# Padding tile rows and ring buffers by 32 and 64 bytes, and moving one small buffer into a ring

## The chip, the cores and the metric

The kernel runs on one core of a Trainium2 chip. The metric is the device time of one execution in microseconds (us), as the median of the runs. The engines are TensorE (PE, with its weight loads as PEld), VectorE (DVE), ScalarE (ACT), GpSimd (POOL) and SyncE (SP), which issues the DMAs.

## The reference, cut to what matters

```python
batch, n_heads, seq, head_dim = (8, 8, 576, 64); n_features = 128      # attention
n_tokens, d_model, d_ff = (4608, 512, 2048)                           # two dense layers, float32 in, float64 weights

def phi(x):                                    # x is q or k, scaled
    h = einsum('bhsd,md->bhsm', x, omega) - sum(x * x, -1) / 2
    return exp(h - max(h, -1)) / sqrt(m)
q_p, k_p = phi(q_s), phi(k_s)
kv = einsum('bhsm,bhsd->bhmd', k_p, v)
z = sum(k_p, axis=2)
attn = einsum('bhsm,bhmd->bhsd', q_p, kv) / (einsum('bhsm,bhm->bhs', q_p, z)[..., None] + 1e-06)

x = attn.transpose(0, 2, 1, 3).reshape(4608, 512)
h = x @ w_in                                   # 512 -> 2048
g = where(h > 0, h, exp(minimum(h, 0)) - 1)
out = g @ w_out                                # 2048 -> 512
```

## The kernel before

The work is recorded as tasks with a cost and a due time. A planner in `Plan.order` simulates the engines, takes on each engine the ready task with the earliest due time, and so writes one fixed order for every engine; the pools' rings (how many buffers a tag has) are part of what it simulates.

All large products use float32 in a form that TensorE takes in one pass and that keeps fewer bits, so each operand is kept as a head (the rounded value) and a tail (what is left). A product is three matmuls: head with head, head with tail, tail with head. In the table below, the moving operand of a matmul is the one that streams through the array, one column after the other, and the other, 128x128, is loaded before as weights; each matmul has its own weight load, which runs beside the matmul before it.

There are three kinds of long streams.

- **Layer 1** (`layer1`, L969 to L971): the weights are blocks of `w1c`, a ring of 3 buffers with 1024 floats each for heads and for tails; the moving operand is 384 columns of `xh` (heads of x) or `xl` (tails). Twelve matmuls make one 128x384 block of h.
- **Layer 2** (`layer2`, L1003 to L1005): the weights are 128x128 pieces of `g`, a ring of 6 buffers; the moving operand is a row `w2h[:, f]` or `w2l[:, f]` of 512 columns.
- **The last form** (`wide1` and `wide2`, L1354, L1324 and L1512): the last 1536 tokens are computed with seven products in place of eight (combined quarter matrices), all with 256 moving columns. Weights are `wp` (in the ring `w1c`), `wq` (in the ring `u`) and `gq` (in the ring `g`; the first product's g has the one buffer `gx` to itself). Moving operands are units kept in `xh` and `xl`, quarters of `w2h` and `w2l`, and combined quarters that `rooms` puts into buffers of other tags (`ld`, `t`, `v`, `qh`, `raw`, `zs`) which the attention no longer needs.

Beside these, the attention projects q and k (`project`, L541): the moving operand is `om`, 256 columns, the weights are blocks of `tk` or `tq`, which lie in the ring `t`.

Three pools share SBUF. Tiles of `const` (`w2h`, `w2l`, `xh`, `xl` among them) come one after the other, then the rings of `sb` in the order in which their tags are first used. So the size of one tile moves every later tile.

Of the kernel before, what the change touches and what calls it, by code (L numbers as in the profile page):

```python
# [9 lines left out]
F32 = mybir.dt.float32  # L10
# [8 lines left out]
P = 128  # L19
# [9 lines left out]
NTT = TB // P  # L29
NBLK = 8  # L30
TOK0 = NBLK * TB
# [36 lines left out]
LAG = 3.4  # L68

# [35 lines left out]
class Buf:  # L105
# [213 lines left out]
def performer_elu_kernel(  # L319
# [41 lines left out]
    w2h = const.tile([P, NF, DM], F32R, name="w2h")  # L361
# [6 lines left out]
    xh = const.tile([P, NC, RING], F32R, name="xh")  # L368
# [587 lines left out]
    def layer1(F, due):  # L956
# [4 lines left out]
        e = Buf(sb, [P, TB], F32, "e", f"e_{F}", 2)  # L961
        g = gt[F] = [Buf(sb, [P, 512], F32R, "g", f"g_{F}_{z}", 6) for z in range(2)]

        def ph():
            return p()[:, 0:TB]

        def mms(c):
            wh, wl = w()[:, 0, c * P:(c + 1) * P], w()[:, 1, c * P:(c + 1) * P]
            nc.tensor.matmul(ph(), wh, xh[:, c, o:o + TB], start=(c == 0), stop=False)  # L969
            nc.tensor.matmul(ph(), wh, xl[:, c, o:o + TB], start=False, stop=False)  # L970
            nc.tensor.matmul(ph(), wl, xh[:, c, o:o + TB], start=False, stop=(c == NC - 1))  # L971

        for c in range(NC):
            reads = [("x3h", SLOT[blk], c), ("x3l", SLOT[blk], c)] if blk > 2 else [(z, k) for k in ring(blk) if k[1] == c for z in ("xh", "xl")]
            op("PE", mm(TB, 3), due + 0.5 * c, lambda c=c: mms(c), [*reads, (w, "h"), (w, "l")], (p, ("f", blk, f)) if c == 0 else (p, ("fl", blk, f)) if c == 3 else (p,))
        due += 2

        op("ACT", act(TB, True), due, lambda: nc.scalar.activation(e(), ph(), AF.Relu, scale=-1.0), (p,), (e,))  # L978
        op("ACT", act(TB), due + 0.2, lambda: nc.scalar.activation(e(), e(), AF.Exp, scale=-1.0), (e,), (e,))  # L979
        op(  # L980
            "DVE", dve(TB), due + 0.8,
            lambda: nc.vector.scalar_tensor_tensor(ph(), e(), -1.0, ph(), ALU.add, ALU.max), (p, e), (p,),  # L982
        )
        first, second = ("ACT", act(TB, True)), ("DVE", dve(TB))
        if blk:
            first, second = second, first
        op(*first, due + 1.2, lambda x: copy(x, g[0]()[:, 0:TB], ph()), (p,), (g[0],), alt=other("g_hi", *second))
        op(
            "DVE", dve(TB), due + 1.5,
            lambda: nc.vector.tensor_tensor(g[1]()[:, 0:TB], ph(), g[0]()[:, 0:TB].bitcast(F32), ALU.subtract),  # L990
# [3 lines left out]
    def layer2(F, due):  # L994
        blk, f, f0, f1 = STEPS[F]
        g = gt.pop(F)
        for tt in range(NTT):
# [14 lines left out]
            r = blk * TB + tt * P  # L1012
# [174 lines left out]
    def std_x(blk, due):  # L1187

        X = [Buf(sb, [P, NJ, M], F32, "h", f"xs_{blk}_{k}", 4) for k in range(2)]

        def x(k):
            return X[k]().rearrange("p j x -> p (j x)")[:, 0:2 * TB].rearrange("p (c x) -> p c x", c=2)

        t0, o = blk * TB, SLOT[blk] * TB
        for k in range(2):
            op(
                "SP", 500, due + 0.1 * k,
                lambda k=k: nc.sync.dma_start(x(k), xd[2 * k:2 * k + 2, :, t0:t0 + TB].rearrange("c p x -> p c x")),
                [("xd", b * NHP + hp) for b in range(B) if b * S < t0 + TB and t0 < b * S + S for hp in (2 * k, 2 * k + 1)]
                + [("f", blk - 1, 11)], (X[k],), P * TB * 8,  # L1200
# [3 lines left out]
            xk = [z[:, 2 * k:2 * k + 2, o:o + TB] for z in (xh, xl)]  # L1204
            heads, tails = ([(nm, SLOT[blk], c) for c in (2 * k, 2 * k + 1)] for nm in ("x3h", "x3l"))
            op(
                "ACT", act(2 * TB), due + UNIT0 + 0.5 * k, lambda e, k=k, xk=xk: copy(e, xk[0], x(k)), (X[k],),
                [*(("xh", z) for z in keys), *heads], alt=other("unit_hi", "DVE", dve(2 * TB, True)), port=True,
            )
            op(  # L1210
                "POOL", pool(2 * TB), due + UNIT0 + 0.4 + 0.5 * k,
# [490 lines left out]
```

## Time and profile before

| | |
|---|---|
| median of 2 runs | 1010.52 us (1010.38 to 1010.66) |
| span of the profiled execution, first to last instruction | 1006.4 us |
| own time of the profiled execution | not listed apart from the two runs; the span is 4.1 us under their median |
| instructions in the span | 24315 |
| PE, PEld busy | 981.2 us (97%), 883.9 us (88%) |
| DVE, ACT, POOL busy | 842.0, 765.8, 557.6 us |
| granted clock of TensorE | full speed (2.4 GHz) in all 40 slices of the page |

The span is what the trace shows; the 4.1 us around it are start and end of the execution. A matmul's duration in the trace holds its way through the array as well as its columns, and matmuls overlap. So what a matmul costs in a stream is the distance from its start to the next start, and the durations tell how two groups of the same shape differ.

### The profile page before, as it was taken

Reading aid. Unit: us, or ns where it says so; the run is one execution under the profiler, and the core shown is the slowest. Engines: PE = TensorE matmul, PEld = TensorE weight load, DVE = VectorE, ACT = ScalarE, POOL = GpSimd, SP = SyncE. Lnnn points to the kernel's source line nnn. Section 1 sums busy time; section 2 is a strip of 40 time slices with the busy share of each in tenths; the row PEclk is TensorE's granted clock in tenths of the full one; section 3 lists DMA queues with packets and bytes.
Section 4 is the critical chain, followed back from the end, with each engine's and each line's share of the span. In section 5 each row is a group of like instructions: output and inputs, shape, how many; then the busy total and the mean of one; then the engine's idle time right before and its main releaser. Section 6 shows DMA issues by size and latency. Waiting matters only on the chain.

```text
span 1006.4 us, 24315 instructions
## 1 busy us (share of the span) xinstructions
PE 981.2 (97%) x7806; PEld 883.9 (88%) x7806; DVE 842.0 (84%) x3077; ACT 765.8 (76%) x2064; POOL 557.6 (55%) x745
## 2 busy tenths in 40 slices
PE   7999999999999999999999999999999999999997
PEld 7788788878888888888888888888789999999997
DVE  7999977887778788878888888889999889779766
ACT  7989777777668888888787778776546788777774
POOL 2667666685547767677577766684442232223221
PEclk9999999999999999999999999999999999999999
DMA  7656787757776776676666766767878876766752
GB/s 230 174 191 198 232 276 262 249 185 236 232 246 202 236 229 204 210 240 207 223 211 220 237 196 211 231 218 236 295 272 309 294 264 205 233 219 193 220 200 66
DMA packets 93264, 226.27 MB, mean 225 GB/s; under 512 B 23056, under 2 KB 35024, under 8 KB 93136
## 3 DMA queue, kind: packets, MB, share of 16 engines
q1 hardware_dynamic: 93136, 224.70, 68.8%
q8 instruction: 63, 1.03, 0.4%
q14 instruction: 65, 0.53, 0.2%
HBM read 187.43 MB, written 37.22 MB: 223 GB/s over the span
## 4 chain that ended last, share of the span: by engine, by line
PE 68%; DVE 15%; DMA 6%; ACT 5%; issue 3%; POOL 3%; SPq 1%; DVEq 0%; POOLq 0%; ACTq 0%
PE acs L1512 9%; PE ph L969 6%; PE ph L971 6%; PE acc L1003 6%; PE ph L970 6%; PE A L1354 6%; PE acc L1005 6%; PE acc L1004 6%; PE B L1354 4%; PE pkv L609 2%; PE pn L829 2%; PE ppq L541 2%; PE ppk L541 2%; DVE junk L727 1%; DVE u_w L914 1%
## 5 line engine op out<-in xcount | busy, mean ns | idle before, releaser
L969 PE MATMUL ph<-xh,w1c 128*128 128x384 f32 x512 | 176.9, 345 | 6.3 <-DVE g L990 4.4
L970 PE MATMUL ph<-xl,w1c 128*128 128x384 f32 x512 | 172.3, 336 | 1.0 <-DVE xl L794 1.0
L971 PE MATMUL ph<-xh,w1c 128*128 128x384 f32 x512 | 172.3, 336 | 0.0
L1003 PE MATMUL acc<-w2h,g 128*128 128x512 f32 x384 | 154.6, 402 | 0.1
L1005 PE MATMUL acc<-w2h,g 128*128 128x512 f32 x384 | 151.6, 395 | 0.0
L1004 PE MATMUL acc<-w2l,g 128*128 128x512 f32 x384 | 151.3, 394 | 0.0
L969 PEld LDWEIGHTS ph<-xh,w1c 128*128 128x128 f32 x512 | 96.2, 188 | 18.7 <-DVE g L990 8.5
L970 PEld LDWEIGHTS ph<-xl,w1c 128*128 128x128 f32 x512 | 96.3, 188 | 3.8 <-DVE xl L794 1.4
L978 ACT ACTIVATE e<-ph 128x384 f32<-128x384 f32 x128 | 62.5, 488 | 47.5 <-PE ph L971 47.0
L381 POOL TENSOR_TENSOR hq<-hq,den 128x512 f32<-128x512 f32 (+1 forms) x96 | 80.9, 852 | 28.7 <-DVE den L736 23.2
L971 PEld LDWEIGHTS ph<-xh,w1c 128*128 128x128 f32 x512 | 96.2, 188 | 0.0
L982 DVE SCALAR_TENSOR_TENSOR ph<-e,ph 128x384 f32<-128x384 f32 x128 | 71.3, 557 | 27.4 <-ACT e L979 26.1
L381 POOL TENSOR_TENSOR gq<-yh,gq 128x256 fp32r<-128x256 f32 x49 | 42.8, 873 | 87.0 <-ACT gq L376 76.8
L1005 PEld LDWEIGHTS acc<-w2h,g 128*128 128x128 f32 x384 | 72.0, 188 | 17.1
L1003 PEld LDWEIGHTS acc<-w2h,g 128*128 128x128 f32 x384 | 72.1, 188 | 16.2 <-issue 6.3
L727 DVE CUSTOM_DVE_ANT_0 junk<-hq,pz 128x128 f32<-128x128 f32 (+1 forms) x320 | 74.6, 279 | 12.7 <-PE pz L705 10.6
L381 POOL TENSOR_TENSOR tk<-xk,tk 64x576 fp32r<-64x576 f32 x45 | 64.1, 1424 | 32.2 <-ACT tk L376 14.9
L461 ACT ACTIVATE hk<-hk,nbk 128x128 f32<-128x128 f32 x216 | 68.4, 391 | 15.7 <-POOL nbk L567 15.3
L1004 PEld LDWEIGHTS acc<-w2l,g 128*128 128x128 f32 x384 | 72.2, 188 | 8.7
L461 ACT ACTIVATE hq<-hq,nbq 128x128 f32<-128x128 f32 x216 | 68.4, 391 | 13.5 <-POOL nbq L567 13.0
L381 POOL TENSOR_TENSOR tq<-xq,tq 64x576 fp32r<-64x576 f32 x46 | 65.9, 1432 | 21.4 <-ACT tq L376 11.1
L990 DVE TENSOR_TENSOR g<-ph,g 128x384 fp32r<-128x384 f32 x128 | 70.6, 551 | 5.7 <-PE pn L829 1.8
(222 smaller groups left out, 2816.9 us busy)
## 6 DMA issues: line engine op xcount, KB each, us to landing
w1c<-w1s SPq DMA_DIRECT2D x112, 512.0 KB, 4.4
wp<-w1t SPq DMA_DIRECT2D x48, 512.0 KB, 3.7
raw_w<-in_w_dram SPq DMA_DIRECT2D x32, 512.0 KB, 4.3
xk<-in_kx_dram SPq DMA_DIRECT2D x24, 576.0 KB, 4.6
xq<-in_qx_dram SPq DMA_DIRECT2D x24, 576.0 KB, 4.6
wp<-w1s SPq DMA_DIRECT2D x24, 512.0 KB, 4.2
v<-in_v_dram SPq DMA_DIRECT2D x32, 325.0 KB, 3.2
w1s<-w1c SPq DMA_DIRECT2D x16, 512.0 KB, 3.9
```

The source lines that it names most:

```text
L381: (nc.vector if e == "DVE" else nc.gpsimd).tensor_tensor(*args)
L461: nc.scalar.activation(h()[:, j, :], src(j), AF.Exp, bias=nb()[:, j:j + 1], scale=-1.0)
L727: nc.vector.tensor_tensor_reduce(out=junk()[r], in0=h()[r, j, :], in1=pz()[r, a * P:(a + 1) * P], scale=1.0, scalar=EPS, op0=ALU.mult, op1 ...
L969: nc.tensor.matmul(ph(), wh, xh[:, c, o:o + TB], start=(c == 0), stop=False)
L970: nc.tensor.matmul(ph(), wh, xl[:, c, o:o + TB], start=False, stop=False)
L971: nc.tensor.matmul(ph(), wl, xh[:, c, o:o + TB], start=False, stop=(c == NC - 1))
L982: lambda: nc.vector.scalar_tensor_tensor(ph(), e(), -1.0, ph(), ALU.add, ALU.max), (p, e), (p,),
L1003: nc.tensor.matmul(a(), g[0]()[:, ts], w2h[:, f], start=(f == f0), stop=False)
L1004: nc.tensor.matmul(a(), g[0]()[:, ts], w2l[:, f], start=False, stop=False)
L1005: nc.tensor.matmul(a(), g[1]()[:, ts], w2h[:, f], start=False, stop=(f == f1 - 1))
L1354: nc.tensor.matmul(o, at(a, i), u[b][:, i], start=(start and fresh_bank and i == 0 and n == 0), stop=(i == 1 and n == 2), skip_group_check ...
L1512: nc.tensor.matmul(bank()[:, z * TH:(z + 1) * TH], g()[:, a * TH + z * P:a * TH + z * P + P], w(b), start=(j == 0 and z == 0 and m == 0), ...
```

## The change

Rows of `w2h` get 8 floats more (32 bytes), of which no one reads the last 8; the same for rows of `xh`. A tile of 64 bytes, `gap`, that no one uses stands between `w2h` and `w2l`. Buffers of the tags `w1c` and `g` get 16 floats more (64 bytes). In the last form the g of the first product takes a buffer of the ring `g`, whose 6 buffers so serve seven g's a step in place of six, and the tag `gx` is gone. The rest of the diff writes the block size as a list in place of one number; all blocks stay 384 tokens.

```diff
+PAD = dict(w1c=16, g=16)
+ROW = 8
...
         if self.tile is None:
             pool, shape, dtype, name = self.args
-            self.tile = pool.tile(shape, dtype, tag=self.key, bufs=self.n, name=name)
+            pad = PAD.get(self.key, 0)
+            if pad:
+                size = 1
+                for n in shape[1:]:
+                    size *= n
+                t = pool.tile([shape[0], size + pad], dtype, tag=self.key, bufs=self.n, name=name)[:, 0:size]
+                self.tile = t if len(shape) == 2 else t.rearrange("p (a x) -> p a x", a=shape[1])
+            else:
+                self.tile = pool.tile(shape, dtype, tag=self.key, bufs=self.n, name=name)
...
-    w2h = const.tile([P, NF, DM], F32R, name="w2h")
+    w2h = const.tile([P, NF, DM + ROW], F32R, name="w2h")[:, :, 0:DM]
+    const.tile([P, 2 * ROW], F32, name="gap")
     w2l = const.tile([P, NF, DM], F32R, name="w2l")
...
-    xh = const.tile([P, NC, RING], F32R, name="xh")
+    xh = const.tile([P, NC, RING + ROW], F32R, name="xh")[:, :, 0:RING]
     xl = const.tile([P, NC, RING], F32R, name="xl")
...
-            tag, n = ("gx", 1) if p == 1 else ("g", 6)
+            tag, n = ("g", 6)
```

The built programs place the tiles at these bytes of a partition. Offsets inside a tile that a matmul starts at are multiples of 256 bytes, but for the rows of the padded tiles, so the start modulo 256 is what the change moves.

| tile | role in a matmul | start before | modulo 256 | start after | modulo 256 |
|---|---|---|---|---|---|
| `om` | moving, projection | 17024 | 128 | 17024 | 128 |
| `w2h` | moving | 19584, rows of 2048 | 128 | 19584, rows of 2080 | 128, 160, 192, 224, 0, 32, 64, 96 in turn |
| `w2l` | moving | 52352 | 128 | 52928 | 192 |
| `xh` | moving | 85120, rows of 4608 | 128 | 85696, rows of 4640 | 192, 224, 0, 32 |
| `xl` | moving | 103552 | 128 | 104256 | 64 |
| `ld` | moving, last form | 123008 | 128 | 123712 | 64 |
| `t` | weights, projection; moving, last form | 132224 | 128 | 132928 | 64 |
| `qh`, `raw` | moving, last form | 146688, 156928 | 0 | 147392, 157632 | 192 |
| `u` (`wq`) | weights | 188800 | 128 | 189504 | 64 |
| `w1c` (`wp`) | weights | 195136, 4096 apart | 64 | 195840, 4160 apart | 0, 64, 128 |
| `g` (`gq`) | weights | 210624, 2048 apart | 192 | 211520, 2112 apart | 64, 128, 192, 0, 64, 128 |
| `gx` | weights | 227264 | 192 | gone | |

Up to the start of the last form every engine has the same instructions in the same order. From there the planner's order differs, since the ring `g` now holds one g more. The first place is on PE, at the head of the last form; `acs` are the banks of the second layer's products, and the number triples are step, product and the buffer's running number. Before:

```order
L1354 MATMUL B<-xh,wp_1_0_11541 128x256 x6
L1512 MATMUL acs_11654<-w2h,gq_0_1_11616 128x256
L1512 MATMUL acs_11654<-w2l,gq_0_1_11616 128x256
L1512 MATMUL acs_11654<-w2h,gq_0_1_11616 128x256 x2
L1512 MATMUL acs_11654<-w2l,gq_0_1_11616 128x256
L1512 MATMUL acs_11654<-w2h,gq_0_1_11616 128x256
L1354 MATMUL A<-xl,wp_1_1_11568 128x256 x6
L1324 MATMUL A<-w2h,gq_0_2_11630 128x256
L1324 MATMUL A<-w2l,gq_0_2_11630 128x256
L1324 MATMUL A<-w2h,gq_0_2_11630 128x256
L1354 MATMUL B<-xl,wp_1_1_11568 128x256 x6
```

The same place on PE after:

```order
L1369 MATMUL B<-xh,wp_1_0_11542 128x256 x6
L1369 MATMUL A<-xl,wp_1_1_11569 128x256 x6
L1339 MATMUL A<-w2h,gq_0_2_11628 128x256
L1339 MATMUL A<-w2l,gq_0_2_11628 128x256
L1339 MATMUL A<-w2h,gq_0_2_11628 128x256
L1527 MATMUL acs_11672<-w2h,gq_0_1_11631 128x256
L1527 MATMUL acs_11672<-w2l,gq_0_1_11631 128x256
L1527 MATMUL acs_11672<-w2h,gq_0_1_11631 128x256 x2
L1527 MATMUL acs_11672<-w2l,gq_0_1_11631 128x256
L1527 MATMUL acs_11672<-w2h,gq_0_1_11631 128x256
L1369 MATMUL B<-xl,wp_1_1_11569 128x256 x6
```

The first product's second-layer matmuls (`gq_0_1`) stand nine matmuls later, behind one product of the next step and half of the second product's.

The second place is on ACT at the same time, where the heads of the g's are written. Before:

```order
L1402 ACTIVATE yh<-c_0_0_11562 128x256
L376 CAST gq_0_1_11616<-yh 128x256
L1407 ACTIVATE yh<-yh 128x256
L376 COPY o_0_0_11625<-acc_0_0_10738 128x512
L376 CAST gq_0_2_11630<-y_0_10_11588 128x256
L1402 ACTIVATE y_0_01_11636<-c_0_0_11534 128x256
```

And after:

```order
L1417 ACTIVATE yh<-c_0_0_11563 128x256
L389 COPY o_0_0_11617<-acc_0_0_10739 128x512
L1422 ACTIVATE yh<-yh 128x256
L389 CAST gq_0_2_11628<-y_0_10_11589 128x256
L389 CAST gq_0_1_11631<-yh 128x256
L1417 ACTIVATE y_0_01_11638<-c_0_0_11535 128x256
```

The first product's g (`gq_0_1`) is written three instructions later, behind the second product's, since it now waits its turn in the ring.

## Rows read from the trace of the kernel before

**Rows 1.** The page, engines: busy us (share of the span) xinstructions.

```profile
PE 981.2 (97%) x7806; PEld 883.9 (88%) x7806; DVE 842.0 (84%) x3077; ACT 765.8 (76%) x2064; POOL 557.6 (55%) x745
```

**Rows 2.** Stretches: us, busy (x) by engine, PEclk, DMA share, GB/s.

```profile
300.00:500.00 200.00, 199.25 (x1756) 175.16 (x1756) 164.21 (x793) 167.22 (x471) 141.37 (x216) 1.00 0.70 220
...
790.00:860.00 70.00, 69.68 (x605) 69.39 (x604) 61.04 (x155) 56.20 (x158) 21.34 (x26) 1.00 0.75 246
```

**Rows 3.** PE's waits, 0 to 790 us: total us, times, longest.

```profile
PE ph L969 <- DVE g L990: 4.4, 8, 1.5
```

**Rows 4.** PE's waits, 790 us to the end, all of them.

```profile
PE A L1354 <- DMA wp<-w1t: 1.2, 1, 1.2
PE acs L1512 <- DVE gq L381: 0.3, 1, 0.3
```

**Rows 5.** By source line: count, duration ns min/median/max, first and last start us.

```profile
L970 PE MATMUL ph<-xl,w1c x512: 332/336/445, 59.0 to 756.3; 128*128 128x384 f32 x171
...
L971 PE MATMUL ph<-xh,w1c x512: 331/336/340, 59.2 to 756.4; 128*128 128x384 f32 x171
...
L1004 PE MATMUL acc<-w2l,g x384: 388/394/398, 72.2 to 769.5; 128*128 128x512 f32 x192
...
L1005 PE MATMUL acc<-w2h,g x384: 388/394/400, 72.4 to 769.7; 128*128 128x512 f32 x192
```

**Rows 6.** Timeline of PE at 698 us: start us, us, instruction.

```profile
698.38 0.39 PE L1004 MATMUL acc<-w2l,g 128*128 128x512 f32 x1
698.62 0.39 PE L1005 MATMUL acc<-w2h,g 128*128 128x512 f32 x1
698.84 0.40 PE L1003 MATMUL acc<-w2h,g 128*128 128x512 f32 x1
...
699.54 0.34 PE L969 MATMUL ph<-xh,w1c 128*128 128x384 f32 x1
...
700.06 0.33 PE L969 MATMUL ph<-xh,w1c 128*128 128x384 f32 x1
...
703.70 0.39 PE L1003 MATMUL acc<-w2h,g 128*128 128x512 f32 x1
```

**Rows 7.** By source line, matmuls of 256 columns, columns as in rows 5.

```profile
L541 PE MATMUL ppk<-om,tk x216: 274/281/359, 109.8 to 670.3; 128*128 128x256 f32 x108
...
L1354 PE MATMUL A<-xh,wp x240: 276/276/357, 758.0 to 986.3; 128*128 128x256 f32 x120
...
L1354 PE MATMUL A<-xl,wq x96: 278/283/384, 764.3 to 991.1; 128*128 128x256 f32 x96
...
L1512 PE MATMUL acs<-w_raw,gq x108: 276/279/384, 834.2 to 1000.1; 128*128 128x256 f32 x108
L1512 PE MATMUL acs<-w_qh,gq x90: 279/279/281, 803.4 to 980.1; 128*128 128x256 f32 x90
...
L1512 PE MATMUL acs<-w_t,gq x72: 276/276/281, 784.5 to 960.5; 128*128 128x256 f32 x72
```

**Rows 8.** Timeline of PE at 926 us, columns as in rows 6.

```profile
926.61 0.87 PE L1512 MATMUL acs<-w_raw,gq 128*128 128x256 f32 x6
927.32 0.87 PE L1354 MATMUL B<-xl,wp 128*128 128x256 f32 x6
928.03 0.87 PE L1354 MATMUL A<-xh,wp 128*128 128x256 f32 x6
...
929.07 0.84 PE L1512 MATMUL acs<-w_ld,gq 128*128 128x256 f32 x6
929.75 0.28 PE L1512 MATMUL acs<-w2h,gq 128*128 128x256 f32 x1
```

**Rows 9.** Tile gq, 790 us to the end: durations; then idle before its instructions.

```profile
L376 ACT CAST gq<-yh x83: 389/407/412, 790.5 to 996.9; 128x256 fp32r<-128x256 f32 x83
...
L381 POOL TENSOR_TENSOR gq<-yh,gq x45: 723/747/1355, 789.5 to 992.6; 128x256 fp32r<-128x256 f32 x45
...
  PE acs L1512: 1.9, 6
```

More of the change, by code (lines that the diff above doesn't have):

```diff
@@ L28 @@
 TB = 384
-NTT = TB // P
-NBLK = 8
-TOK0 = NBLK * TB
+BLOCKS = [TB] * 8
+NBLK = len(BLOCKS)
+START = [sum(BLOCKS[:n]) for n in range(NBLK + 1)]
+TOK0 = START[-1]
 SB = 512
@@ L976, in layer1 @@
         due += 2
-        op("ACT", act(TB, True), due, lambda: nc.scalar.activation(e(), ph(), AF.Relu, scale=-1.0), (p,), (e,))
-        op("ACT", act(TB), due + 0.2, lambda: nc.scalar.activation(e(), e(), AF.Exp, scale=-1.0), (e,), (e,))
-        op(
-            "DVE", dve(TB), due + 0.8,
-            lambda: nc.vector.scalar_tensor_tensor(ph(), e(), -1.0, ph(), ALU.add, ALU.max), (p, e), (p,),
+        op("ACT", act(n, True), due, lambda: nc.scalar.activation(e()[:, 0:n], ph(), AF.Relu, scale=-1.0), (p,), (e,))
@@ L983, in layer1 @@
+        op("ACT", act(n), due + 0.2, lambda: nc.scalar.activation(e()[:, 0:n], e()[:, 0:n], AF.Exp, scale=-1.0), (e,), (e,))
+        op(
+            "DVE", dve(n), due + 0.8,
+            lambda: nc.vector.scalar_tensor_tensor(ph(), e()[:, 0:n], -1.0, ph(), ALU.add, ALU.max), (p, e), (p,),
         )
-        first, second = ("ACT", act(TB, True)), ("DVE", dve(TB))
+        first, second = ("ACT", act(n, True)), ("DVE", dve(n))
         if blk:
             first, second = second, first
-        op(*first, due + 1.2, lambda x: copy(x, g[0]()[:, 0:TB], ph()), (p,), (g[0],), alt=other("g_hi", *second))
+        op(*first, due + 1.2, lambda x: copy(x, g[0]()[:, 0:n], ph()), (p,), (g[0],), alt=other("g_hi", *second))
@@ L996, in layer2 @@
         g = gt.pop(F)
-        for tt in range(NTT):
+        for tt in range(BLOCKS[blk] // P):
             if f == f0:
@@ L1203, in std_x @@
             keys = [z for z in ring(SLOT[blk]) if z[1] in (2 * k, 2 * k + 1)] if first else []
-            xk = [z[:, 2 * k:2 * k + 2, o:o + TB] for z in (xh, xl)]
+            xk = [z[:, 2 * k:2 * k + 2, o:o + n] for z in (xh, xl)]
             heads, tails = ([(nm, SLOT[blk], c) for c in (2 * k, 2 * k + 1)] for nm in ("x3h", "x3l"))
             op(
-                "ACT", act(2 * TB), due + UNIT0 + 0.5 * k, lambda e, k=k, xk=xk: copy(e, xk[0], x(k)), (X[k],),
-                [*(("xh", z) for z in keys), *heads], alt=other("unit_hi", "DVE", dve(2 * TB, True)), port=True,
+                "ACT", act(2 * n), due + UNIT0 + 0.5 * k, lambda e, k=k, xk=xk: copy(e, xk[0], x(k)), (X[k],),
+                [*(("xh", z) for z in keys), *heads], alt=other("unit_hi", "DVE", dve(2 * n, True)), port=True,
             )
             op(
-                "POOL", pool(2 * TB), due + UNIT0 + 0.4 + 0.5 * k,
+                "POOL", pool(2 * n), due + UNIT0 + 0.4 + 0.5 * k,
                 lambda e, k=k, xk=xk: tt(e, xk[1], x(k), xk[0].bitcast(F32), ALU.subtract), (X[k], *heads),
-                [*(("xl", z) for z in keys), *tails], alt=other("unit", "DVE", dve(2 * TB)), port=True,
+                [*(("xl", z) for z in keys), *tails], alt=other("unit", "DVE", dve(2 * n)), port=True,
             )
```

28 lines of the change are left out of this document (15 added, 13 removed).

## The prediction, before the changed kernel ran

> **What bounds the kernel now.** I read the page's engine line first. PE is busy 97% of the span, DVE 84%, and nothing else comes near [rows 1]. Then the stretches: from 300 to 500 us PE is busy 199.25 of 200 us, and in the last form 69.68 of 70, at full clock in both [rows 2]. Then PE's waits, for whether that busy time is broken up: ahead of 790 us the largest is 4.4 us in 8 pieces, and in the last form there are 1.5 us in all [rows 3, 4]. So matmuls set the time, and a change that leaves their number alone can act only through how far apart their starts lie, or by making waits.
>
> So the next view is the timeline, for the distance of starts. In a row of 21 matmuls of 384 columns it is 3.64 us / 21 = 173.3 ns, and for 512 columns 0.70 us / 3 = 233.3 ns [rows 6]. At 2.4 GHz, one column a cycle, 384 and 512 columns take 160.0 and 213.3 ns. So 13.3 and 20.0 ns of each matmul are neither columns nor waits. The same for 256 columns: six matmuls from `w_ld` take 0.68 us, 113.3 ns each, six from `w_raw` 0.71 us, 118.3 ns [rows 8]; the columns alone take 106.7 ns.
>
> These extra ns depend on which tiles are read. Same shape, same line, only other buffers: the median is 276 ns with `w_t` or with `xh` and `wp`, 279 with `w_raw` and `w_qh`, 283 with `xl` and `wq`, 281 with `om` and `tk` [rows 7]. Beside the table of start bytes that reads: moving at 128 and weights at 64 or 192 (modulo 256) give 276; moving at 0 gives 279; both at 128 give 281 to 283. It also has a memory: six matmuls of `xl` and `wp` right behind `w_raw` keep 118 ns (0.71 us for six), and after `w_ld` the distance is 113 again [rows 8]. Almost all of layer 1 and 2 has moving 128 with weights 64 or 192, so for the long streams the trace of before shows one placing alone.
>
> **The change part by part.** The padded floats are read by no one, the number of instructions is the same, and no transfer gets longer. What remains is four terms.
>
> *Projection (L541).* 432 matmuls read `om` at 128 and weights at 128, median 281. Their weights move to 64, a pair that shows 276 elsewhere [rows 7]: 432 x -5 ns = -2.2 us, of which I count -2, since PE is busy 199.25 of 200 us there [rows 2].
>
> *The last form.* There are 1008 + 864 + 144 = 2016 matmuls of 256 columns here. From the operands of the two programs I count those whose moving start and whose next weights are equal modulo 256: 156 before, 444 after. At 7 ns each (283 against 276, rows 7) the 288 more cost +2.0 us. Another 198 leave the place 0 (279 to at best 276): -0.6. In 407 the moving start becomes an odd multiple of 32, for which no row has a price: 0 in the middle, and 7 ns either way would be 2.8 us. Sum +1.
>
> *The long streams.* 1536 matmuls of 384 columns and 1152 of 512. All of them get other starts, and no row has a price. The bounds: below, all of the extra goes, 1536 x 13.3 + 1152 x 20.0 = 20.4 + 23.0 = -43 us; above, each takes the 7 ns that a coinciding pair costs at 256 columns: 2688 x 7 = +19 us. Inside that, the nearest rows are these streams' own fastest: minimum 331 against median 336, and 388 against 394 [rows 5]. These are met at the start of a stream (0.22 us from 698.62 to 698.84 at 512 columns, then 233 in the settled run, rows 6), that is, where the start offset has just changed or the stream has just begun. Now heads and tails start at different offsets and the rows of heads differ among themselves by 32 bytes, so a stream is in that state more often. If all reached the minimum it were 1536 x 5 + 1152 x 6 = 14.6 us; I take half, -7. That is a choice between bounds and no measurement.
>
> *The ring and the order.* In the last form seven g's a step share 6 buffers. What could be late is a g's head on ACT and its tail on POOL, 407 and 747 ns [rows 9], behind the release of a buffer. Instructions that write or read a g waited 1.9 us in all for PE's second-layer matmuls, 6 times in the whole stage [rows 9], PE waited 0.3 us for a g [rows 4], and the new order puts the first product's matmuls nine matmuls later, which gives that g more time. Queued behind such a wait on ACT are the next heads and the copies out of the banks, for which PE waits. I put it at 0; the cover is that PE has other products to run meanwhile, and without it the price is in the fourth case below. SP's weight loads change places by one or two in the queue only.
>
> Sum: -2 + 1 - 7 + 0 = -8 us. The profiled span is 1006.4 us, and the median 4.1 us above it; nothing in the change touches start or end, so 998.4 + 4.1 = 1002.5 us.
>
> **The rivals.** *Nothing moves.* The extra ns of the long streams may belong to their length: 6.7, 13.3 and 20.0 ns at 256, 384 and 512 columns grow by the same 6.7 ns for each 128 columns, as a cost tied to columns would. Then only the first two terms are left, which is 1009.5; I give 1007 to 1014. For it speaks that straight line, against it that at 256 columns placing does count (276 against 283, rows 7). The Trainium skill would have it so too: SBUF — State Buffer, section "SBUF: two separate sides", says that on the engine side only the port shared by VectorE and GpSimd causes contention and that PE waits for no one. By that page padding is worth nothing at all and the time is 1010.5; rows 7 disagree with it by 7 ns a matmul, for 256 columns.
>
> *The extra goes.* If what costs is two streams that meet in one place, and rows 32 bytes apart keep them from meeting, most of the 43 us can go; at 0.7 of it, -30 us, the time is 980. For it speaks that placing costs at all; against it that starts coincide more often after the change than before (444 against 156 in the last form). [...]
>
> *They meet more often* (slower). The same mechanism with the other sign, in layers 1 and 2: before, nearly all pairs there are in the best class that the trace shows. After, `xl` at 64 meets `w1c`'s second buffer at 64, `w2l` at 192 meets `g`'s third at 192, and a state lasts into matmuls behind it [rows 8]. If half of the 2688 take 7 ns more that is +9.4, with the last form's +1 and the projection's -2 some +9: 1019. It decides from about a third of the pairs on, where it outweighs the gains. The upper end is +19, 1029.
>
> *The ring runs dry* (slower). If a g's buffer is released less than 407 + 747 = 1.15 us ahead of its use, PE stands for up to that long once a step; 24 steps make 28 us at most, and half of it +14, 1016. Against it: the waits of rows 4 and 9 are near nothing.
>
> **How the numbers follow.** Forecast (992 to 1007) 0.36; nothing moves 0.24; the extra goes (968 to 992) 0.20; they meet more often (1014 to 1029) 0.15; the ring runs dry 0.05. The predicted time is the likeliest case's, 1002.5; its own range is 992 to 1007. The range 980 to 1020 leaves out half of the third case and the upper halves of the last two, together somewhat under 0.2. 2% is 20 us, about what a measurement of this kernel can tell from no change: faster by more (under 990.3) is nearly all of the third case, 0.19; slower by more (over 1030.7) only the far ends of the last two, 0.03; within, 0.78.
>
> **What would show it.** The first sign is the distance of starts in a settled run: 173.3 and 233.3 would fall to about 171 and 230 by the forecast, stay by the first rival, go under 168 and 224 by the second, rise to 177 and 237 by the third. The median of L541 should come to 276. `xl` with `wq` (both at 64 now) should stay at 283, since these coincide again; if it falls, equal starts are not what costs. PE's waits in the last form should stay under 3 us; the fourth case would show there, as PE waiting for `gq`. The prediction is wrong as a whole if the long streams' distance moves by more than 6 ns, either way, since then a placing that the trace of before nowhere shows decides the time.

## The result, and the profile after

The changed kernel took 1020.93 us (median of 2 runs, 1018.84 to 1023.02) against 1010.52: 1.0104 times as long, 95% interval 1.0055 to 1.0153. It is about 10 us slower, where 8 us faster was forecast. On another chip, beside the experiments, it took 1019.48 us against 1008.75, a ratio of 1.0104 (1.0077 to 1.0130).

The profiled span is 1017.1 us against 1006.4, 10.7 us more. To find the stretch in which they arise, take the first start of the group that opens the last form (`A<-xh,wp`) and the last start of the group that closes it (`acs<-w2h,gq`). By source line, the columns as in [rows 5, 7]; first the kernel before, the group that starts last:

```profile
L1512 PE MATMUL acs<-w2h,gq x288: 276/276/284, 770.6 to 1000.8; 128*128 128x256 f32 x144
```

The kernel after, the same view (L1369, L1527, L554, L985 and L1019 are the lines that were L1354, L1512, L541, L971 and L1005):

```profile
L1369 PE MATMUL A<-xh,wp x240: 275/281/392, 758.3 to 996.9; 128*128 128x256 f32 x120
...
L1369 PE MATMUL A<-xl,wq x96: 274/282/384, 764.6 to 1001.8; 128*128 128x256 f32 x96
...
L1527 PE MATMUL acs<-w2h,gq x288: 274/280/385, 772.0 to 1010.9; 128*128 128x256 f32 x144
...
L1527 PE MATMUL acs<-w_raw,gq x108: 274/281/387, 839.2 to 1009.5; 128*128 128x256 f32 x108
...
L1527 PE MATMUL acs<-w_t,gq x72: 274/279/290, 788.8 to 963.6; 128*128 128x256 f32 x72
...
L554 PE MATMUL ppk<-om,tk x216: 275/279/385, 110.3 to 670.4; 128*128 128x256 f32 x108
...
L985 PE MATMUL ph<-xh,w1c x512: 331/337/346, 59.7 to 756.7; 128*128 128x384 f32 x171
...
L1019 PE MATMUL acc<-w2h,g x384: 387/394/408, 73.0 to 770.0; 128*128 128x512 f32 x192
```

The last form begins at 758.3 us, before at 758.0 [rows 7]: 0.3 of the 10.7 us lie ahead of it. From there to the start of the last matmul it takes 1010.9 - 758.3 = 252.6 us, before 1000.8 - 758.0 = 242.8: 9.8 us. Behind the last matmul's start lie 6.2 us in place of 5.6. This length, 242.8 before, is the measure of all that follows, since it leaves out what happens earlier.

The same rows tell half of the reason. Groups that stood at 276 ns before [rows 7] now stand at 279 to 282, whichever tile they read. The long streams stand nearly where they were: 337 ns after 336, 394 as before [rows 5]. Three stretches of the kernel after, columns as in [rows 2]:

```profile
790.00:860.00 70.00, 68.25 (x566) 67.02 (x565) 57.74 (x148) 51.98 (x147) 21.32 (x27) 1.00 0.70 229
...
880.00:920.00 40.00, 40.00 (x342) 40.00 (x341) 28.24 (x77) 29.89 (x81) 9.31 (x13) 1.00 0.63 205
...
1004.00:1011.00 7.00, 6.68 (x51) 5.95 (x49) 6.10 (x14) 3.30 (x9) 1.97 (x3) 1.00 0.03 10
```

And of the kernel before, the second one, and its own last 7 us:

```profile
880.00:920.00 40.00, 40.00 (x348) 40.00 (x348) 34.21 (x85) 30.46 (x83) 10.69 (x12) 1.00 0.64 209
...
994.00:1001.00 7.00, 7.00 (x62) 6.92 (x60) 6.43 (x14) 2.42 (x7) 1.47 (x2) 1.00 0.12 41
```

From 880 to 920 us PE is busy for 40.00 of 40 us in both, at full clock, and yet starts 342 matmuls against 348: 117.0 ns a matmul against 114.9. A busy share of 100% hid that. From 790 to 860 us both things are seen: PE is busy 1.43 us less than before [rows 2], a wait, and starts 566 matmuls against 605. In the last 7 us it starts 51 against 62, and PE is busy for 6.68 us of them in place of 7.00: waits again.

The settled distances, from the timeline of PE in the kernel after (columns as in [rows 6]):

```profile
698.48 0.39 PE L1018 MATMUL acc<-w2l,g 128*128 128x512 f32 x1
...
699.64 0.34 PE L983 MATMUL ph<-xh,w1c 128*128 128x384 f32 x1
...
703.85 0.40 PE L1017 MATMUL acc<-w2h,g 128*128 128x512 f32 x1
...
935.69 0.88 PE L1369 MATMUL A<-xh,wp 128*128 128x256 f32 x6
936.41 0.29 PE L1527 MATMUL acs<-w2h,gq 128*128 128x256 f32 x1
...
938.18 0.84 PE L1527 MATMUL acs<-w_ld,gq 128*128 128x256 f32 x6
938.86 0.98 PE L1369 MATMUL A<-xl,wp 128*128 128x256 f32 x6
```

24 matmuls of 384 columns take 4.21 us, 175.4 ns each, against 173.3 [rows 6]; five of 512 columns 1.16 us, 232 against 233.3. Six of `xh` and `wp` take 0.72 us, 120 ns; six of `w_ld` still 0.68, 113.3, as in [rows 8]. So 256 columns pay, and in sum the long streams hardly do.

PE's waits of the kernel after from 757 us on, all of them:

```profile
PE A L1369 <- ACT c L389: 1.9, 5, 0.5
PE B L1369 <- DVE B L1324: 1.9, 2, 1.6
PE acs L1527 <- ACT gq L389: 0.2, 1, 0.2
```

In the kernel before the same view has 2.8 us: beside the two waits of [rows 4] these two.

```profile
PE B L1354 <- DVE B L1309: 0.8, 2, 0.4
PE A L1354 <- ACT c L376: 0.5, 1, 0.5
```

PE waits for banks that ACT and DVE empty, and hardly for a g. The theory formed from this: two costs that add, the ring (waits) and the starts (distance). Its rivals are that the ring does it all and that the starts do.

### The profile page after: what moved, and what is told of

It reads as the page before. It is cut to its first block, busy times and chain, and to the rows that moved or that the text cites. A ratio compares the mean times of both kernels' runs of the same rounds, so it can differ in the third digit from the quotient of the medians.

```text
span 1017.1 us, 24297 instructions
## 1 busy us (share of the span) xinstructions
PE 989.3 (97%) x7806; PEld 891.3 (88%) x7806; DVE 838.3 (82%) x3068; ACT 767.4 (75%) x2064; POOL 560.4 (55%) x754
## 4 chain that ended last, share of the span: by engine, by line
PE 67%; DVE 16%; ACT 6%; DMA 5%; issue 3%; POOL 2%; SPq 0%; DVEq 0%; POOLq 0%; ACTq 0%
PE acs L1527 8%; PE ph L983 7%; PE acc L1017 6%; PE ph L985 6%; PE ph L984 6%; PE acc L1019 6%; PE acc L1018 6%; PE A L1369 5%; PE B L1369 4%; PE pkv L622 2%; PE pn L842 2%; PE ppq L554 2%; PE ppk L554 2%; DVE rw L394 1%; DVE u_w L927 1%
## 5 line engine op out<-in xcount | busy, mean ns | idle before, releaser
L985 PE MATMUL ph<-xh,w1c 128*128 128x384 f32 x512 | 172.8, 337 | 0.0
L1019 PE MATMUL acc<-w2h,g 128*128 128x512 f32 x384 | 151.3, 394 | 0.0
L394 POOL TENSOR_TENSOR gq<-y,gq 128x256 fp32r<-128x256 f32 x30 | 24.4, 815 | 165.1 <-ACT gq L389 148.1
L985 PEld LDWEIGHTS ph<-xh,w1c 128*128 128x128 f32 x512 | 96.1, 188 | 0.0
L1019 PEld LDWEIGHTS acc<-w2h,g 128*128 128x128 f32 x384 | 72.1, 188 | 17.2 <-DVE g L1004 0.2
L740 DVE CUSTOM_DVE_ANT_0 junk<-hq,pz 128x128 f32<-128x128 f32 (+1 forms) x320 | 74.5, 278 | 12.9 <-PE pz L718 10.7
L474 ACT ACTIVATE hk<-hk,nbk 128x128 f32<-128x128 f32 x216 | 68.4, 391 | 16.1 <-POOL nbk L580 15.7
L394 POOL TENSOR_TENSOR tq<-xq,tq 64x576 fp32r<-64x576 f32 x46 | 65.8, 1430 | 22.6 <-ACT tq L389 10.3
```

What stands on the lines that cost most here:

```text
L394: (nc.vector if e == "DVE" else nc.gpsimd).tensor_tensor(*args)
L474: nc.scalar.activation(h()[:, j, :], src(j), AF.Exp, bias=nb()[:, j:j + 1], scale=-1.0)
L740: nc.vector.tensor_tensor_reduce(out=junk()[r], in0=h()[r, j, :], in1=pz()[r, a * P:(a + 1) * P], scale=1.0, scalar=EPS, op0=ALU.mult, op1 ...
L985: nc.tensor.matmul(ph(), wl, xh[:, c, o:o + n], start=False, stop=(c == NC - 1))
L1019: nc.tensor.matmul(a(), g[1]()[:, ts], w2h[:, f], start=False, stop=(f == f1 - 1))
```

## The experiments

"Length" is from the first start of `A<-xh,wp` to the last start of `acs<-w2h,gq` in a kernel's own profile. Executions differ in their first 60 us (345 to 405 matmuls start there, in some at a granted clock of 0.94 to 0.99 in the mean), which shifts where the last form begins; the length leaves that out. "Distance" and "waits" split the length, worked out from the starts in the trace: for each of the 2015 matmuls of 256 columns, the time to the next start less the 106.7 ns of its columns counts as distance if it is under 45 ns, else as a wait; each is a sum in us. What they leave of the length is the same in all kernels: 214.9 us for the columns and 6.2 to 6.5 us for 27 matmuls of 512 columns that still run there. "In 40 us" is the number of matmuls in a stretch of 40.00 busy us (880 to 920, or 890 to 930 where the last form begins some 15 us later).

| kernel | order | last form from, to | length | distance | waits | in 40 us | median | ratio to before (95%) |
|---|---|---|---|---|---|---|---|---|
| before | its own | 758.0, 1000.8 | 242.8 | 16.9 | 4.8 | 348 | 1010.52 | |
| after | ring's | 758.3, 1010.9 | 252.6 | 22.6 | 8.8 | 342 | 1020.93 | 1.0104 (1.0055 to 1.0153) |
| e1 ring only | ring's | 762.7, 1010.8 | 248.1 | 16.8 | 9.9 | 352 | 1018.49 | 1.0075 (1.0049 to 1.0101) |
| e2 weights padded | before's | 775.9, 1023.3 | 247.4 | 22.8 | 3.3 | 341 | 1030.96 | 1.0214 (1.0188 to 1.0240) |
| e3 all coincide | before's | 774.7, 1022.5 | 247.8 | 23.2 | 3.4 | 341 | 1028.87 | 1.0189 (1.0158 to 1.0219) |
| e4 apart everywhere | before's | 776.3, 1016.4 | 240.1 | 14.5 | 4.3 | | 1023.13 | 1.0129 (1.0103 to 1.0155) |
| e5 ring, rows | ring's | 760.4, 1012.1 | 251.7 | 22.1 | 8.4 | 343 | 1019.51 | 1.0091 (1.0073 to 1.0109) |
| e7 apart by moving | before's | 760.8, 1000.8 | 240.0 | 14.4 | 4.3 | 355 | 1007.13 | 0.9979 (0.9958 to 1.0000) |
| e8 own buffer | ring's | 764.5, 1013.1 | 248.6 | 17.1 | 10.3 | | 1018.97 | 1.0080 (1.0057 to 1.0103) |
| e9 all shifted by 32 | before's | 762.6, 1004.8 | 242.2 | 17.0 | 3.9 | 350 | 1009.32 | 0.9983 (0.9964 to 1.0002) |
| e10 ring, shifted by 64 | ring's | 765.2, 1013.0 | 247.8 | 16.8 | 9.9 | 352 | 1020.03 | 1.0071 (1.0040 to 1.0101) |
| e11 ring, g by 128 | ring's | 763.1, 1014.3 | 251.2 | 17.7 | 12.3 | 350 | 1017.88 | 1.0078 (1.0048 to 1.0107) |
| e12 ring, g by 64 | ring's | 762.0, 1013.1 | 251.1 | 20.9 | 8.8 | 345 | 1017.39 | 1.0074 (1.0044 to 1.0104) |
| e13 one junk | before's | 773.5, 1015.6 | 242.1 | 16.8 | 4.0 | | 1023.21 | 1.0155 (1.0130 to 1.0181) |
| e14 ring, old order | before's | 758.7, 1009.0 | 250.3 | 17.1 | 12.1 | | 1018.01 | 1.0090 (1.0062 to 1.0117) |
| e15 ring of seven | a third | 767.9, 1016.7 | 248.8 | 16.7 | 10.9 | | 1024.85 | 1.0171 (1.0144 to 1.0197) |
| e16 after again | ring's | 759.4, 1013.0 | 253.6 | 22.5 | 9.8 | | 1019.48 | 1.0104 (1.0077 to 1.0130) |

Line numbers in the rows below are each kernel's own; they differ from before's by a few lines' shift.

### The ring by itself (e1)

```diff
-            tag, n = ("gx", 1) if p == 1 else ("g", 6)
+            tag, n = ("g", 6)
```

> The first product's g takes turns in the ring g, nothing is padded: every engine has the order of the changed kernel, every tile the start of the kernel before. Theory A (the spread of start offsets costs some 3 ns on each of the 2000 matmuls of 256 columns in the last form, the ring and the new order cost some 4 us of waits there): 1014.5 us, the distance of starts of 256 columns in the last form back at about 115 ns as before. Rival B (it is the ring and the order alone): 1020 us. Rival C (the ring costs nothing): 1010.5 us.

Measured: 1018.49 us. The kernel with the ring alone, by source line, its waits of PE from 757 us on, and its stretch:

```profile
L1354 PE MATMUL A<-xh,wp x240: 276/276/393, 762.7 to 996.9; 128*128 128x256 f32 x120
...
L1512 PE MATMUL acs<-w2h,gq x288: 276/276/385, 776.8 to 1010.8; 128*128 128x256 f32 x144
```

```profile
PE A L1354 <- ACT c L376: 2.5, 7, 0.6
PE B L1354 <- DVE B L1309: 1.8, 2, 1.6
```

```profile
880.00:920.00 40.00, 40.00 (x352) 40.00 (x351) 28.36 (x77) 30.25 (x83) 10.28 (x14) 1.00 0.68 220
```

The medians are back at 276 ns and PE starts 352 matmuls in 40 us, but the length is 248.1: the ring alone costs 5.3 us, nearly all of it in waits (9.9 us against 4.8). The two above, the same as in the kernel after, are 4.3 of the 5.2 us that the view shows. It shows less than the starts do, for two reasons. It counts idle time from the end of the matmul before, and a matmul of 276 ns ends some 160 ns after the next could have started. And the first matmul behind a longer wait is itself long (the maxima of 384 to 393 ns in the rows by source line): the next starts 212 to 235 ns behind it, 18 times in e1, 14 in after and 5 in before, some 107 ns more each than in a settled run. The median is 8.6 us above before, with an interval of 4.9 to 10.2, which holds the 5.3.

### Other starts, in before's order (e2 to e4)

Room for gaps came from one ring: the unused output `junk` of the attention's row sums got one buffer in place of two. e13 below shows what that did; the last form has no `junk`.

```diff
+PAD = dict(w1c=8, g=16)                            (e2, used as in the change)
+    const.tile([P, 16], F32, name="gap")            (e3, behind xl)
+GAP = dict(qh=32, u=16, w1c=16)                     (e4, unused tiles ahead of these rings;)
+    const.tile([P, 16] ...), const.tile([P, 48] ...)   (and two in const)
-                    junk = Buf(sb, [P, M], F32, "junk", f"junk_{i}_{j}_{a}", 2)
+                    junk = Buf(sb, [P, M], F32, "junk", f"junk_{i}_{j}_{a}", 1)
```

Starts modulo 256. e2: moving as before, weights 64, 96, 128 (`wp`) and 32, 96, 160, 224 (`gq`). e3: `xh`, `xl` at 128 with `wp` at 128, so that 848 pairs of a moving start and the next weights coincide (156 in before); `gq` at 0. e4: nearly all moving of the last form at 128, all weights at 64 or 192 (25 pairs coincide).

> Only the weights' buffers are padded (w1c by 32 bytes, g by 64, so that weights start at 64, 96, 128 and at 32, 96, 160, 224 modulo 256), gx stays, and the ring junk has one buffer to make room; every engine has the order of before. Theory A (what costs is that the offsets change from matmul to matmul): 256 columns in the last form rise from 115 to 118 ns, 2000 x 3 = +6 us, 1016 us. Rival B (ring and order alone): 1010.5 us. Rival D (what costs is only that the moving start and the next weights coincide): one w1c buffer in three coincides, 336 x 7 ns = +2.4 us, 1013 us.

> A tile of 64 bytes behind xl shifts all that follows, so that weights of layer 1 and of the first half of the last form (w1c, 128) start where xh and xl do (128), everywhere and always; g goes to 0; junk has one buffer; order of before. Theory A (changing offsets cost): a settled run is as fast as ever, 1010 us. Rival D (coinciding starts cost): L1354 at 283 ns in place of 276, 1008 x 7 = +7 us, and layer 1 some 2.4 ns for each of 1536, +3.7: 1018 to 1021 us.

> Small gaps put every moving operand at 128 (om at 192) and every weight at 64 or 192 (tk and tq at 128), so that the placings which showed 279 to 283 ns before are gone (wq with xh and xl, w_raw and w_qh, om with tk and tq); junk has one buffer; order of before. Theories A and D: 144 x 7 + 198 x 3.3 ns = 1.7 us, as much again where matmuls behind them kept the slow distance, and 432 x 5 ns = 2 us in the projection: 1005 us. Rival B (placing does not count for the time): 1010.5 us.

All three medians miss, since the last form begins some 17 us later (775.9, 774.7 and 776.3 us against 758.0), which no theory had. The last form tells them apart nonetheless: 247.4, 247.8 and 240.1 us. e2 and e3, 890 to 930 us:

```profile
890.00:930.00 40.00, 40.00 (x341) 40.00 (x340) 31.53 (x81) 29.48 (x81) 9.35 (x13) 1.00 0.67 217
```

```profile
890.00:930.00 40.00, 40.00 (x341) 40.00 (x340) 31.73 (x81) 29.52 (x81) 9.16 (x12) 1.00 0.66 214
```

So the starts alone, with before's order and before's `gx`, cost 4.6 to 5.0 us, in distance (22.8 and 23.2 us against 16.9), and e4's starts gain 2.7. Starts that change from buffer to buffer (e2) and one start for each tile with many pairs that coincide (e3) cost the same. That ends the theory that only changing starts cost. In e2 424 pairs coincide too, but it isn't these alone: more than 20 matmuls behind the last such pair the distance is still 11.0 ns over the columns on average (523 distances), in the kernel after 11.1 (222), and in before 7.7 (1335).

### The control (e13)

```diff
-                    junk = Buf(sb, [P, M], F32, "junk", f"junk_{i}_{j}_{a}", 2)
+                    junk = Buf(sb, [P, M], F32, "junk", f"junk_{i}_{j}_{a}", 1)
```

> A control: the kernel before with one buffer in place of two for the unused output of the row sums, and nothing else; order and start offsets modulo 256 as before. The three kernels with other placings had this too, for room. Theory J (it is what made their stages ahead of the last form longer): the last form starts 13 to 15 us later, its own length stays at 243 us, 1023 to 1025 us. Rival (their gaps and pads did that): 1010.

Measured: 1023.21 us, length 242.1, last form from 773.5. Groups of DVE, first of the kernel before, then of the control (busy us, mean ns of one | idle before):

```profile
L727 DVE CUSTOM_DVE_ANT_0 junk<-hq,pz 128x128 f32<-128x128 f32 (+1 forms) x320 | 74.6, 279 | 12.7 <-PE pz L705 10.6 <-ACT hq L461 0.9 <-PE pz L708 0.5
```

```profile
L727 DVE CUSTOM_DVE_ANT_0 junk<-hq,pz 128x128 f32<-128x128 f32 (+1 forms) x320 | 90.3, 282 | 21.6 <-PE pz L705 9.8 <-ACT hq L461 0.3
```

One of them lasts as long as before (279 and 282 ns), but the 320 together take 15.7 us more: with two buffers the next starts while the last still ends, with one it does not. The timeline of DVE shows the starts, two neighbours of the kernel before and then of the control:

```profile
80.65 0.28 DVE L727 CUSTOM_DVE_ANT_0 junk<-hq,pz 128x128 f32<-128x128 f32 x1
80.88 0.29 DVE L727 CUSTOM_DVE_ANT_0 junk<-hq,pz 128x128 f32<-128x128 f32 x1
```

```profile
85.61 0.29 DVE L727 CUSTOM_DVE_ANT_0 junk<-hq,pz 128x128 f32<-128x128 f32 x1
86.05 0.29 DVE L727 CUSTOM_DVE_ANT_0 junk<-hq,pz 128x128 f32<-128x128 f32 x1
```

These are 0.23 and 0.44 us apart; over all 239 neighbours of one group the mean is 219 ns before and 337 in the control. The busy time holds only the lost overlap; the rest is idle time between them. This is most of what shifted e2 to e4: their own last forms begin 1 to 3 us behind the control's. Against the control (1.0155) the medians show the starts as well: e2 1.0214, e3 1.0189, e4 1.0129, which is some 6 and 3 us more and 3 us less; only e2's interval lies apart from the control's.

### The heads' rows alone, and a placing without any byte (e5, e7)

e5 is the change with `PAD = {}`: the ring, the 32 bytes a row and the 64 bytes between `w2h` and `w2l`, which also shift what follows; no padding of `w1c` and `g`.

> The change without the 64 bytes behind the buffers of layer 1's weights and of g: the ring and the 32 bytes behind the heads' rows stay, so all weights of one tile keep one start (0 and 128 modulo 256), but the moving rows of heads start at 192, 224, 0 and 32. Theory S (256-column matmuls keep the 113 ns only where all moving starts are 128 and all weights' starts 64 or 192 modulo 256; one tile elsewhere slows those behind it too): 117 to 119 ns in the last form, as after the change, 1019 to 1021 us. Rival W (only the weights' start changing from buffer to buffer costs): 113 to 114 ns, 1015 us. Both: the ring's waits stay, PE stands 8 to 10 us in the last form.

e7 is before with the small rings `nbk` and `z` taken first ahead of `qh` and `u`:

```diff
+AHEAD = dict(qh=("nbk", 9), u=("z", 2))
...
+            first = AHEAD.pop(self.key, None)
+            if first:
+                for z in range(2):
+                    pool.tile([shape[0], first[1]], F32, tag=first[0], bufs=2, name=f"ahead_{first[0]}{z}")
```

> The kernel before with two rings of small tiles placed elsewhere, no byte more, the same order: the unpacked copies and the second unit's heads move from 0 to 128, the third weight piece from 128 to 192, so every moving operand of the last form starts at 128 and every weight at 64 or 192 modulo 256. Theory S: the last form's extra over the columns falls from 16.9 us to 14 to 15, all else stays, 1008 us. Rival J (what slowed the kernel with the wider gaps was the wider gaps and not its single buffer for the sums' unused output): 1015 to 1023. Rival (placing of these tiles is worth nothing): 1010.

e5: 1019.51 us, length 251.7. e7: 1007.13, length 240.0. Their stretches, e5 first:

```profile
880.00:920.00 40.00, 40.00 (x343) 40.00 (x342) 28.23 (x76) 29.57 (x81) 9.26 (x13) 1.00 0.66 211
```

```profile
880.00:920.00 40.00, 40.00 (x355) 40.00 (x354) 33.53 (x85) 30.14 (x83) 11.97 (x14) 1.00 0.71 226
```

Padding the rows, with the shifts that it brings, is enough for nearly the whole price of the starts (343 against after's 342, distance 22.1 against 22.6 us); padding the weights is enough too (e2); they don't add. The other way, 355 matmuls at 112.7 ns, is the best that was found: e7 is the fastest kernel here, 2.6 us under before on the same chip, though its interval just reaches 1. By source line, e7's `w_raw`, which had 279 ns at start 0 [rows 7], has 276 at 128:

```profile
L1518 PE MATMUL acs<-w_raw,gq x108: 276/276/388, 837.0 to 1000.1; 128*128 128x256 f32 x108
```

### Is it the place or the difference? (e9, e10)

Both put an unused tile ahead of all others, 32 bytes in before (e9) and 64 bytes in the kernel with the ring alone (e10).

```diff
+    const.tile([P, 8], F32, name="gap")      (e9;  16 in e10)
     ident = const.tile([P, P], F32, name="ident")
```

> The kernel before with 32 bytes ahead of all its tiles and nothing else: all starts shift by 32, moving at 160 and weights at 96 and 224 modulo 256, all differences as before, the same order. Theory S1 (what counts is the difference of moving start and weight start): nothing changes, 113 to 114 ns in the last form, 1010 us. Theory S2 (what counts is where a start lies by itself, 128 for the moving one, 64 or 192 for the weights): 117 to 119 ns, the extra of the last form rises from 16.9 to 22 or 23 us, 1015 to 1016 us.

> The ring alone (same order as after the change), with 64 bytes ahead of all tiles: moving at 192, weights at 128 and 0 modulo 256, every difference as with the ring alone. It goes further than the shift by 32, which left each start within its own 64 bytes. Theory S1 (differences count): extra of the last form stays at 16.8 us, 1018 us like the ring alone. Theory S2 (the place itself counts, in pieces of 64 bytes): extra 22 to 23 us, 1023 to 1024.

e9: 1009.32 us, length 242.2, 350 matmuls. e10: 1020.03, length 247.8, and its stretch equals that of e1:

```profile
880.00:920.00 40.00, 40.00 (x352) 40.00 (x351) 28.06 (x77) 29.68 (x82) 10.43 (x15) 1.00 0.70 221
```

Nothing moves in either. As far as shifts of 32 and 64 bytes show it, where a start lies by itself does not count; how starts lie to each other does.

### The change's own padding of g, and twice as much (e11, e12)

The ring alone, with 32 or 16 floats more behind each g:

```diff
+            if self.key == "g":
+                self.tile = pool.tile([P, 512 + GPAD], dtype, tag="g", bufs=6, name=name)[:, 0:512]
```

> The ring alone, with 128 bytes behind each of the six g buffers: they start at 192 and 64 in turn, modulo 256, all else as with the ring alone. Theory S (moving at 128 with weights at 64 or 192 is fast, in any mixture): extra of the last form 16 to 17 us, 113 to 114 ns, 1018 us. Rival V (any change of the weights' start from buffer to buffer costs): extra 20 to 23 us, 1022 to 1024.

> The ring alone, with 64 bytes behind each of the six g buffers, which is the change's own padding of g and nothing else of it: starts 192, 0, 64, 128, 192, 0 modulo 256. Theory S: three of the six buffers lie off 64 and 192, and the slow state lasts into what follows: extra of the last form 20 to 23 us, 117 ns and more, 1022 to 1024. Rival (only equal starts cost, one buffer in six): extra 17 to 18 us, 1019.

Medians 1017.88 and 1017.39, alike and like e1's: the runs cannot tell them apart. The profiles can. By source line, e11 and e12:

```profile
L1517 PE MATMUL acs<-w2h,gq x288: 276/276/415, 776.9 to 1014.3; 128*128 128x256 f32 x144
```

```profile
L1517 PE MATMUL acs<-w2h,gq x288: 274/280/385, 776.1 to 1013.1; 128*128 128x256 f32 x144
```

Their stretches, e11 and e12:

```profile
880.00:920.00 40.00, 40.00 (x350) 40.00 (x349) 28.25 (x78) 29.35 (x81) 9.39 (x14) 1.00 0.69 215
```

```profile
880.00:920.00 40.00, 40.00 (x345) 40.00 (x344) 28.18 (x77) 29.33 (x81) 9.79 (x14) 1.00 0.67 212
```

Starts in turn at 192 and 64 keep 276 ns (350 in 40 us); starts at 192, 0, 64 and 128 have 280 (345). The lengths don't show it, since e11's profiled execution has a granted clock of 0.83 between 783 and 793 us. By distance e12 pays 4.1 us over e1 and e11 0.9. That e12's 3.0 us of length over e1 do not appear in its median stays unexplained; as a difference to before its interval is 4.4 to 10.5 us, wide enough for them.

### Buffers or order? (e8, e14, e15)

e8 lets the planner count the first product's g in the ring but gives it a buffer of its own; e14 is the reverse, before's order with that g in the ring's buffers:

```diff
+            tag, n = ("gx", 1) if self.own else (self.key, self.n)       (e8; own where p == 1)
+            tag, n = ("g", 6) if self.key == "gx" else (self.key, self.n)   (e14)
             self.tile = pool.tile(shape, dtype, tag=tag, bufs=n, name=name)
```

> The ring's order without the ring: the planner still lets the first product's g take turns in the g buffers, so every engine has the order of the changed kernel, but that g gets its own buffer, as in the kernel before; starts as before. Theory R1 (what costs in the ring is that a buffer comes free too late): PE's waits in the last form fall from 9.9 us back to 5, 1010 to 1012 us. Theory R2 (what costs is the order that the planner makes of the ring, a tail on POOL instead of DVE and the first product's matmuls last): waits stay at 9 to 10 us, 1015 to 1018.

> The reverse of the kernel with the ring's order and a buffer of its own: every engine has the order of the kernel before, but the first product's g really takes turns in the six g buffers and its former buffer is gone. Theory R2 (the planner's order is what costs): PE's waits in the last form stay at about 5 us, 1010 us. Theory R1 (buffers come free too late): waits of 10 us and more, 1016 to 1020.

e8: 1018.97 us, length 248.6, so the order alone has the ring's whole price (5.8 us); its waits of PE from 757 us on begin:

```profile
PE A L1356 <- ACT c L378: 2.6, 7, 0.6
PE B L1356 <- DVE B L1311: 2.0, 2, 1.6
```

e14: 1018.01 us, length 250.3, so the buffers alone cost 7.5. Its wait of ACT:

```profile
ACT gq L377 <- PE acs L1513: 14.3, 23, 1.0
```

Neither theory holds alone. In before's order ACT stands 14.3 us until PE has released a g (before 1.9 us in six waits, of all engines [rows 9]), and its copies out of the banks stand behind that in its order. The planner sees this coming and writes an order without that wait (in e1, e8 and after ACT has none of its kind), and this order costs nearly as much: 10.3 us of waits in e8 against 12.1 in e14.

> All g's in one ring as after the change, but of seven buffers, which takes the same bytes as six and one apart before; starts as before; the planner's order differs from layer 1 on. Theory R (six buffers for seven g's a step cost, not the sharing): the last form takes 243 us again, 1008 to 1011 us unless the new order costs something ahead of it. Rival (any shared ring costs): the last form takes 248 us and more, 1015.

e15 (7 in place of 6 in both places where the ring is made): 1024.85 us, length 248.8. The rival held: a seventh buffer, and so the old number of bytes, does not give the 5 us back. Here the planner's order is another from layer 1 on, and the last form starts at 767.9 us, 9.9 later than in before. So a seventh buffer does not mend the planner's order; since the order is another one too, e15 does not price the buffer by itself.

### The whole again (e16)

> The changed kernel itself beside the others on one chip. If the ring (+5.3 us of the last form's length by the ring alone) and the starts (+4.7 by padding alone) simply add, the last form takes 253 us and the time is 10 us above before, 1020; if the two overlap it is 5 to 7 us above.

1019.48 us, length 253.6. Ring (248.1 - 242.8 = 5.3) and starts (4.6 to 5.0) add up to 9.9 to 10.3, measured 9.8 and 10.8: the two halves add. The change's own starts were not run in before's order: e2 and e3 are other placings with the same distance, and beside the ring the change's starts cost 4.5 and 5.5 us (252.6 and 253.6 - 248.1). The medians agree with the sum but do not show the split: by them the kernels with the ring's order and before's distances (e1, e8, e10) are 7 to 8 us above before, with intervals from 4 to 10, and after 10.5.

## Why the prediction was wrong

**What bounds the kernel** was right: PE, through the distance of starts and through waits, and both did it. That 256 columns, and so the last form, are where placing counts stood in [rows 7, 8]. The waits of the last form were read too small: the view has 1.5 us from 790 us on, by the starts of the matmuls it is 4.8 in the whole form.

**The projection**, -2 us: the median went from 281 to 279 and not to 276, 432 x -2 ns = -0.9 us. Right in sign; "a pair that shows 276 elsewhere" was not enough.

**The last form's starts**, +1 us: this is the first step that failed. It priced coinciding pairs alone (288 more, 7 ns each) and put the odd multiples of 32 at 0, 2.8 us at most. What the runs show is that a matmul pays without coinciding itself: in after all groups stand at 279 to 282 ns, in e2 too, and either padding alone has nearly the whole effect. In its place the runs show +4.6 to +5.0 (e2, e3), beside the ring +4.5 and +5.5. [rows 8] held the warning: six matmuls of `xl` and `wp`, a fast pair, kept 118 ns behind `w_raw`. The longer distance carries over; so a tile in a bad place is not priced by its own matmuls, and where starts change all the time few runs of matmuls settle at 113 ns.

**The long streams**, -7 us: the second step that failed. "A stream is in that state more often", drawn from the first distances of a stream, was not so: 384 columns went from 173.3 to 175.4 ns and 512 from 233.3 to 232, and the last form began at 758.3 in place of 758.0, so all terms ahead of it, the projection's among them, sum to about 0. In this "nothing moves" was right. On average over all of them, 384 columns cost 1.1 ns more and 512 0.6 ns less, 1536 x 1.1 - 1152 x 0.6 = about +1 us in place of -7.

**The ring and the order**, 0 us: the third. "The cover is that PE has other products to run meanwhile": e1 prices it at 5.3 us of length. [rows 4, 9] showed a ring nearly without waits, but the ring before had one g less to serve and an order made for that; e8 shows that the new order costs without any shared buffer. The prediction named the mechanism (copies out of the banks behind a wait on ACT) and asked what is queued behind; it took the shown waits, 0.3 and 1.9 us, as the price of a ring that they did not belong to. The end shows the new plan as well: 51 matmuls in the last 7 us against 62.

**The rivals.** "They meet more often" (1019) and "the ring runs dry" (1016) came nearest in time, but each for half of the cause at most, so that nearness is luck. The first put the place in layers 1 and 2, where it was not, and its mechanism, that streams meet in one place, is at most a part: pairs that lie 64 and 192 bytes apart, which did well in before, have 10.9 and 10.5 ns over their columns on average in after, against 8.7 and 7.5, and more than 20 matmuls behind any pair that coincides the matmuls of after still have 11.1, against 7.7 in before. The second had PE standing until a g's buffer is released; in after PE waits 0.2 us for `gq`, and such a wait is large only in e14, in before's order, 14.3 us on ACT. "The extra goes" has no support: the smallest mean distance that any placing gave here over a stretch of 40 us is 112.7 ns for 256 columns (e7), 6 ns over the columns alone. The Trainium skill says in SBUF — State Buffer, section "SBUF: two separate sides", that PE never waits on anyone on the engine side; taken as the prediction took it, that the place of a tile is worth nothing to PE, it does not hold here: 341 (e2) and 355 (e7) matmuls in 40 busy us against 348 before. Whether it is at the port that the time goes, no run shows.

**The signs.** `xl` with `wq` stayed (283 to 282), but since the other groups rose to 279 to 282, that tells nothing of coincidence. PE's waits in the last form were to stay under 3 us; the view gives 4.0 from 757 us on, nearly all for banks, 0.2 for `gq`. The long streams moved by 2.1 and 1.3 ns, far from the 6 ns that were to show the prediction wrong as a whole: only the sign of the waits pointed at the last form, where it failed.

**Left open**: what it is in the relation of starts that decides. It is unchanged by shifts of all tiles by 32 and 64 bytes; moving and weights 64 or 192 apart with nearly all moving alike is fast (e4, e7), weights in turn 128 apart nearly so (e11, 350), 64 apart not (e12, 345). Yet `w_raw` at 0 with g at 192 is slow and `xh` at 128 with `wp` at 64 fast, with the same difference. What in the ring's order makes banks late, e8 and e15 do not say either. One lead, not tested: from 757 us on ACT has a wait in after, e1, e8 and e15, whose order was planned with the shared ring, that before and e14 have not; here in after:

```profile
ACT gq L389 <- POOL yh L394: 4.1, 3, 1.9
```

## What to carry to other kernels

Price a tile's place by what stands behind it as well, and price a change of places by running the placing alone: count matmuls in a stretch where PE is 100% busy, since the busy share does not see the distance. A ring that serves one more user is another plan, not the old plan with a wait; the old waits say nothing of it, and the bytes saved (2 KB here) were not free. Where places matter, moving small tiles (e7) did without bytes and without a new order what padding did not: 2.8 us less in the last form, though the interval of its median reaches no change.

## What the runs showed of the hardware

- The distance of 256-column matmuls depends on how the starts of the operands lie to each other (112.7 ns on average over 40 us in e7, 114.9 in before, 117.3 in e2 and e3); shifts of all starts by 32 and 64 bytes change nothing (e9, e10). For 384 and 512 columns no placing tried here moved the mean by more than about 1.3 ns (e5, 384 columns).
- A slow distance carries over into matmuls in a fast placing (118 ns for six of `xl` and `wp` behind `w_raw` [rows 8]).
- A wait of PE often costs more than its own length: behind it the first distance of starts is some 222 ns in place of 115 (14 times in the last form of after, 5 in before).
- In this kernel, neighbouring row sums on DVE that write one buffer start 337 ns apart on average, with two buffers in turn 219, though nothing reads the buffer: 15.7 us more busy time and some 12 us more idle time in 320 instructions (e13), which cost the kernel 14.5 us.
